# Transposes of 15 chunks as 32x32 blocks on DVE with copies on the DMA queues, instead of on PE

## The chip, the core and the metric

One NeuronCore of one Trainium2 chip runs the whole kernel. The metric is the device time of one execution in microseconds (us). Engines are named as in the profile: PE (TensorE matmuls), PEld (its weight loads), DVE (VectorE), ACT (ScalarE), POOL (GpSimd) and SP (SyncE, which issues all DMAs here from one queue, in order). A difference under 0.3% (2.9 us) is what a measurement of this kernel cannot tell from none.

## What is computed

Shapes: batch 4, 8 heads, sequence 576, head width 64, so 2304 tokens of width 512.

```python
x = attention(q, k, v)                       # local band of 7 plus a 4x down-sampled attention
# block 1: layer norm and a channel MLP of width 2048
xn = (x - mu) / sqrt(var + 1e-6) * g_ln
x2 = x + relu(xn @ w_ch1) @ w_ch2            # 512 -> 2048 -> 512
# block 2: token MLP of width 256 over the 576 tokens of a batch, then a channel MLP of width 1536
u  = x2 + (relu(x2.T @ w_tok1) @ w_tok2).T
out = u + relu(u @ w_ch1b) @ w_ch2b          # 512 -> 1536 -> 512
```

## The kernel before

The 2304 tokens are 18 tiles of 128, taken two at a time as **chunks** of 256. Block 1 works on chunks 0 to 8, block 2 on the same tokens as chunks 9 to 17. All large products run in fp32r on a high and a low part of each operand, three matmuls (`PASSES`) for one product.

The spine is a list of 252 **units**, one for each chunk and each 128 columns of the hidden width: 16 units a chunk in block 1 (`UA`), 12 in block 2 (`UB`). In a unit, `g1` does 12 matmuls of 256 columns into a PSUM tile `h`, ACT and DVE turn it into the high and low part of `ht` (ReLU), and `g2` does 6 matmuls of 512 columns that add into two accumulators. `g1` of the next unit is issued ahead of `g2` of this one, so `ht` has one unit's time to become ready. `base[c]` is the number of the first unit of chunk c.

`g1` needs the chunk's activations transposed, in `xT[c]` (128 channels by 4 by 2 parts by 256 tokens; two buffers, so chunk c can be written when the last `g1` of chunk c-2 has read). For each of the two tiles of a chunk, `xt_transpose` issues four 128x128 transposes on PE into one PSUM bank; `xt_hi` (ACT) writes the high part from there, `xt_lo` (DVE) the low part.

Everything else is hung into the spine by `put(pos, f)`, at a place counted in units: attention of the later batches (`LATER`), layer norm (`ln_center`), the token product of a batch (`tok1`, over 5 tiles of tokens, the fifth only 64 rows, then `tok_relu` and `tok2`), and the weights. Those are 64-bit in DRAM; `split_unit` turns each piece (128x512, two pieces to a unit) by three DVE steps, an ACT and a DVE step into high and low parts. The weights of block 2 (24 pieces, tensor `wb`) are loaded through two staging buffers `st` while chunks 8 and 9 run, since they take the buffers of block 1's weights as those come free.

`put` sets priorities; the framework's scheduler then places each instruction on its engine's queue when it expects its inputs to be there. Each engine, SP among them, runs its queue strictly in order. SP takes its DMAs' counters in turn from a set of eight.

Of the kernel before, what the change touches and what calls it, by code (L numbers as in the profile page):

```python
# [7 lines left out]
F32 = mybir.dt.float32  # L8
F32R = mybir.dt.float32r
I32 = mybir.dt.int32  # L10
ACTF = mybir.ActivationFunctionType
ALU = mybir.AluOpType
# [4 lines left out]
DM = H * D  # L17
# [3 lines left out]
CT = 2  # L21
CN = CT * 128
NCH = NTILE // CT
KD = DM // 128
# [7 lines left out]
DT = 256  # L32
# [2 lines left out]
QW = 512  # L35
T2P = 288
PASSES = ((0, 0), (0, 1), (1, 0))
XSP = 50
HP2 = 300
START_PAIRS = 5  # L40
SETS = 3
# [24 lines left out]
    td_copy 4 1  # L66
"""

LATER = ((1, 25), (27, 56), (57, 87))


def tile_of(b, tl):
    g = 9 * (b // 2)
    if tl == 4:
        return g + 4
    return g + tl + (5 if b % 2 else 0)
# [16 lines left out]
def block_kernel(ctx: ExitStack, tc: tile.TileContext, qk, vw, vg, g_ln, wa, t1, t2, wb, band, out):  # L93
    nc = tc.nc
# [7 lines left out]
    xt_p = ctx.enter_context(tc.tile_pool(name="xt_p", bufs=2))  # L102
    ht_p = ctx.enter_context(tc.tile_pool(name="ht_p", bufs=2))
    x_p = ctx.enter_context(tc.tile_pool(name="x_p", bufs=5))
# [9 lines left out]
    x2_scr = [dram.tile([128, CT, DM], F32, name=f"x2_scr{c}") for c in range(NCH)]  # L114
# [11 lines left out]
    def psg(tag=None):  # L126
        if tag is None:
            turn[0] += 1
            tag = rota[turn[0] % len(rota)]
        return POOLS[tag].tile([128, 512], F32, tag=tag, name=tag)  # L130

    def f32(ap):
        return ap.bitcast(F32)
# [5 lines left out]
    wa, wb, t1, t2 = (w.bitcast(I32) for w in (wa, wb, t1, t2))  # L139
# [392 lines left out]
    xT = {}  # L532
    mvs = {}
    rstd = {}
    xcs = {}
# [35 lines left out]
    def xt_transpose(c, j, src):  # L571
        ps = psg()
        for kk in range(KD):
            nc.tensor.transpose(ps[:, kk * 128:(kk + 1) * 128], src[:, kk * 128:(kk + 1) * 128], ident)  # L574
        xps[c, j] = ps.rearrange("p (k n) -> p k n", k=KD)

    def xt_hi(c, j):
        if c not in xT:
            xT[c] = xt_p.tile([128, KD, 2, CN], F32R, tag="xt", name="xt")
        n = slice(j * 128, (j + 1) * 128)  # L580
        nc.scalar.activation(out=xT[c][:, :, 0, n], in_=xps[c, j], func=ACTF.Copy)  # L581

    def xt_lo(c, j):
        n = slice(j * 128, (j + 1) * 128)
        nc.vector.tensor_tensor(  # L585
            out=xT[c][:, :, 1, n], in0=xps.pop((c, j)), in1=f32(xT[c][:, :, 0, n]), op=ALU.subtract
        )

    def xt_split(c, j):
        with tc.high_priority(offset=XSP):  # L590
            xt_hi(c, j)
            xt_lo(c, j)


    def nunits(c):
# [57 lines left out]
    uch = {}  # L653
    tokw = {}
# [29 lines left out]
    def xs_load(b, n):  # L684
        t = tok["pool"].tile([128, DM], F32, tag="xr", name="xr", bufs=1)
        k = tile_of(b, n)
        nc.sync.dma_start(out=t, in_=x2_scr[k // CT][:, k % CT])
        xs[b, n] = t

    def xs_split(b, n):  # L690
# [6 lines left out]
    rps = {}  # L697
    r_t = {}

    def tok1(b, n):  # L700
        t = xs.pop((b, n))
        rows = slice(64 * (b % 2), 64 * (b % 2) + 64) if n == 4 else slice(0, 128)
        for m in range(DT // 128):
            if n == 0:
                rps[b, m] = psg("k")
            for i, (a, e) in enumerate(PASSES):
                nc.tensor.matmul(  # L707
                    out=rps[b, m], lhsT=tokw["t1"][rows, a, n, m * 128:(m + 1) * 128], rhs=t[rows, e, :],
                    start=(n == 0 and i == 0), stop=(n == 4 and i == 2),
                )  # L710

    def tok_relu(b):
        r = wp.tile([128, DT // 128, 2, DM], F32R, tag="w", name="r")
# [39 lines left out]
    def put(pos, f, *args):  # L753
        u, half = divmod(int(2 * pos), 2)
        u = min(u, NSEQ - 1)
        (bg if half else mid)[u].append(lambda: f(*args))

    def put_prep1(c, e):
        for j in range(CT):
            put(e - 5.5 + j, ln_center, c, j)  # L760
            put(e - 3.5 + j, lambda c=c, j=j: xt_transpose(c, j, xcs.pop((c, j))))
            put(e - 3 + j, xt_split, c, j)
        put(e + 4, ln_rstd, c)

    def put_tok(b, u):
        for n in range(5):
            put(u + n, xs_load, b, n)
            put(u + 1 + n, xs_split, b, n)
            put(u + 2 + n, tok1, b, n)
        put(u + 6.5, tok_relu, b)  # L770

    def put_prep2(c, e):
        put(e - 7, u_load, c)
        for j in range(CT):
            put(e - 5 + 0.5 * j, tok2, c, j)
            put(e - 3.5 + j, lambda c=c, j=j: xt_transpose(c, j, uch[c][:, j]))
            put(e - 3 + j, xt_split, c, j)


    pieces = [(i, part) for i in range(UA) for part in range(NPC)]  # L780
# [54 lines left out]
    def conv_step(k):  # L835
# [6 lines left out]
    steps = {f.__name__: f for f in (  # L842
        q_sums, v_sums, s_max, s_exp, d_max, d_exp, t_pe, t_copy, td_pe, td_copy, avd_pe, avd_norm, up_write,
        up_read, av_pe, av_norm, load, fill, consts, ln_center, xt_pe, xt_hi, xt_lo,
    )}
    steps.update(
# [39 lines left out]
    for n in range(START_PAIRS, len(order) + 1):  # L886
        a = [(f, n) for f in (a_scores, a_down, a_turn, a_turn_down)] if n < len(order) else []
        v = [(f, n - 1) for f in (a_values_down, a_values)] if n > START_PAIRS else []
        later += a[:1] + v[:1] + a[1:2] + v[1:] + a[2:]
    o = 0  # L890
    for i, (u0, u1) in enumerate(LATER):
        e = later.index((a_values, NP * (i + 2) - 1)) + 1
        for k, (f, n) in enumerate(later[o:e]):
            put(u0 + k * (u1 - u0) / (e - o), f, n)
        o = e
    for c in range(2, NCH):
        put_prep1(c, base[c] - 1)
# [23 lines left out]
    for c in range(NCH, 2 * NCH):  # L921
        put_prep2(c, base[c] - 1)
# [97 lines left out]
```

## Time and profile before

| | |
|---|---|
| median of 3 runs | 961.3 us (960.32 to 963.04) |
| the profiled execution's own time | 960.96 us |
| its span in the profile | 958.8 us |
| mean granted clock of PE | 0.989 of 2.4 GHz |

The span is what the rows further down divide; 2.2 us lie around it.

### The profile page before, as it was taken

The page shows a single profiled execution, that of the slowest core. Times are in us where ns is not written, and L with a number is a line of the kernel's source. Part 1 is how long each engine was busy: PE and PEld are TensorE (multiplying, and loading weights), DVE is VectorE, ACT ScalarE, POOL GpSimd, SP SyncE. Part 2 cuts the span into 40 slices and gives each one's busy share as a digit, 9 for nine tenths or more (in the row PEclk, how much of TensorE's full clock was granted, in tenths as well). Part 3 has the DMA queues.
Part 4 walks back from the last instruction along what each step waited for, and adds up shares of the span by engine and source line. Part 5 has one row for each costly group of instructions (what it writes and reads, how often), then busy time and mean ns, then how long its engine had stood idle before and what let it go on. Part 6 is the DMA issues. An engine that isn't in the chain of part 4 may idle for free.

```text
span 958.8 us, 16724 instructions
## 1 busy us (share of the span) xinstructions
PE 926.9 (97%) x6822; PEld 813.5 (85%) x6822; DVE 430.8 (45%) x1014; ACT 279.5 (29%) x809; POOL 148.8 (16%) x176
## 2 busy tenths in 40 slices
PE   7978999899999999999999999999999999999998
PEld 5767788788988889888889988888888988899997
DVE  4786888873333423366322268982222213122211
ACT  5444354434433334332121123221121111111111
POOL 6453214312123220120110011001000010000000
PEclk9799999999999999999999999999999999999999
DMA  8654565632131320234110135531101010000000
GB/s 220 182 184 138 151 194 159 186 95 77 53 94 57 98 63 18 92 103 150 33 44 23 44 111 168 190 126 66 56 12 44 23 45 23 1 23 1 23 23 23
DMA packets 43932, 81.85 MB, mean 85 GB/s; under 512 B 4080, under 2 KB 22768, under 8 KB 43856
## 3 DMA queue, kind: packets, MB, share of 16 engines
q1 hardware_dynamic: 43856, 80.79, 27.1%
q8 instruction: 54, 0.88, 0.4%
q14 instruction: 22, 0.18, 0.1%
HBM read 66.62 MB, written 14.16 MB: 84 GB/s over the span
## 4 chain that ended last, share of the span: by engine, by line
PE 76%; DMA 10%; DVE 9%; ACT 2%; issue 1%; POOL 1%; SPq 1%; DVEq 0%; ACTq 0%; POOLq 0%
PE h L615 31%; PE acc L636 30%; DMA st<-in_wb_dram 3%; PE g L738 2%; DVE cv L160 2%; PE k L707 2%; DMA xr<-x_scr 2%; PE k L636 2%; DMA up_scr<-od 2%; DVE cv L155 1%; DVE w L168 1%; PE g L574 1%; PE g L283 1%; PE g L364 1%; PE g L469 1%
## 5 line engine op out<-in xcount | busy, mean ns | idle before, releaser
L615 PEld LDWEIGHTS h<-xt,w 128*128 128x128 f32 x3024 | 396.5, 191 | 25.2 <-ACT w L165 1.9
L615 PE MATMUL h<-xt,w 128*128 128x256 f32 x3024 | 414.2, 285 | 2.3 <-ACT w L165 1.7
L636 PE MATMUL acc<-w,ht 128*128 128x512 f32 x1416 | 380.6, 400 | 7.3 <-ACT ht L621 4.3
L636 PEld LDWEIGHTS acc<-w,ht 128*128 128x128 f32 x1416 | 251.9, 189 | 59.8 <-ACT ht L621 6.2
L622 DVE SCALAR_TENSOR_TENSOR ht<-h,ht 128x256 fp32r<-128x256 f32 x252 | 106.1, 422 | 411.7 <-ACT ht L621 411.4
L621 ACT ACTIVATE ht<-h 128x256 fp32r<-128x256 f32 x252 | 96.6, 384 | 433.0 <-PE h L615 423.2
L694 POOL TENSOR_TENSOR xs<-xr,xs 128x512 fp32r<-128x512 f32 x20 | 27.6, 1380 | 338.3 <-ACT xs L693 338.3
L347 POOL TENSOR_TENSOR vg<-vg 72x256 f32<-72x256 f32 x39 | 31.6, 810 | 168.7 <-DMA vg<-in_vg_dram 129.7
L165 ACT ACTIVATE w<-cv 128x512 fp32r<-128x512 f32 x56 | 35.5, 634 | 72.4 <-DVE cv L160 72.2
L168 DVE TENSOR_TENSOR w<-cv,w 128x512 fp32r<-128x512 f32 x56 | 43.2, 775 | 9.4 <-ACT w L165 9.2
L155 DVE SCALAR_TENSOR_TENSOR cv<-st,cv 128x512 int32<-128x512 int32 (+4 forms) x63 | 42.8, 682 | 0.8
L160 DVE SCALAR_TENSOR_TENSOR cv<-st,cv 128x512 int32<-128x512 int32 (+4 forms) x63 | 42.4, 675 | 0.6
L516 POOL TENSOR_TENSOR x<-x,pt 128x256 f32<-128x256 f32 (+2 forms) x44 | 28.1, 651 | 65.6 <-ACT pt L503 55.7
L707 PE MATMUL k<-xs,t1w 128*128 128x512 f32 (+1 forms) x120 | 35.7, 404 | 0.0
L738 PE MATMUL g<-r,t2w 128*128 128x512 f32 x120 | 34.4, 396 | 0.0
L150 DVE TENSOR_SCALAR cv<-st 128x512 int32<-128x512 int32 (+4 forms) x63 | 25.5, 406 | 12.8 <-DMA st<-in_wb_dram 6.2
L636 PE MATMUL k<-w,ht 128*128 128x512 f32 x96 | 27.7, 406 | 0.1
L585 DVE TENSOR_TENSOR xt<-g,xt 128x512 fp32r<-128x512 f32 x28 | 19.2, 687 | 12.9 <-ACT xt L581 12.3
L707 PEld LDWEIGHTS k<-xs,t1w 128*128 128x128 f32 (+1 forms) x120 | 20.6, 188 | 3.9 <-issue 0.6
L503 ACT ACTIVATE pt<-g,rz 128x64 f32<-128x64 f32 (+1 forms) x78 | 17.5, 323 | 21.9 <-DVE rz L493 21.8
L738 PEld LDWEIGHTS g<-r,t2w 128*128 128x128 f32 x120 | 21.0, 189 | 3.2 <-issue 0.2
L301 ACT ACTIVATE sm<-g,nm 128x70 f32<-128x70 f32 x80 | 18.1, 349 | 12.1 <-DVE nm L293 12.1
(162 smaller groups left out, 713.7 us busy)
## 6 DMA issues: line engine op xcount, KB each, us to landing
st<-in_wa_dram SPq DMA_DIRECT2D x28, 512.0 KB
st<-in_wb_dram SPq DMA_DIRECT2D x24, 512.0 KB
qk<-in_qk_dram SPq DMA_DIRECT2D x13, 579.0 KB
xr<-x_scr SPq DMA_DIRECT2D x20, 256.0 KB
x_scr<-x SPq DMA_DIRECT2D x18, 256.0 KB
x<-x_scr SPq DMA_DIRECT2D x9, 512.0 KB
out_dram<-x SPq DMA_DIRECT2D x18, 256.0 KB
vw<-in_vw_dram SPq DMA_DIRECT2D x13, 319.9 KB
```

The costliest lines, as they stand in the source:

```text
L155: nc.vector.scalar_tensor_tensor(out=f, in0=h, scalar=-0x40000000, in1=f, op0=ALU.bitwise_and, op1=ALU.bitwise_or)
L160: nc.vector.scalar_tensor_tensor(out=f, in0=l, scalar=29, in1=f, op0=ALU.logical_shift_right, op1=ALU.bitwise_or)
L165: nc.scalar.activation(out=hi, in_=f.bitcast(F32), func=ACTF.Copy)
L168: nc.vector.tensor_tensor(out=lo, in0=f.bitcast(F32), in1=f32(hi), op=ALU.subtract)
L347: nc.gpsimd.tensor_tensor(out=vd[:, :, :, :D], in0=vd[:, :, :, :D], in1=vgt[:, :, o:o + 128].rearrange("p c (h d) -> p c h d", h=2), op=AL ...
L516: (eng or nc.gpsimd).tensor_tensor(out=x, in0=x, in1=tmp[rows, tl:tl + k].rearrange("p t h d -> p t (h d)"), op=ALU.add)
L615: nc.tensor.matmul(out=hp[:, :CN], lhsT=w[:, 0, a, kk * 128:(kk + 1) * 128], rhs=xT[c][:, kk, e, :], start=(n == 0), stop=(n == 3 * KD - 1),)
L621: nc.scalar.activation(out=t[:, 0], in_=hp[:, :CN], func=ACTF.Relu)
L622: nc.vector.scalar_tensor_tensor(out=t[:, 1], in0=hp[:, :CN], scalar=0.0, in1=f32(t[:, 0]), op0=ALU.max, op1=ALU.subtract)
L636: nc.tensor.matmul(out=acc[c, j], lhsT=t[:, a, j * 128:(j + 1) * 128], rhs=w[:, 1, e, :], start=(m == 0 and n == 0), stop=(last and n == 2),)
L707: nc.tensor.matmul(out=rps[b, m], lhsT=tokw["t1"][rows, a, n, m * 128:(m + 1) * 128], rhs=t[rows, e, :], start=(n == 0 and i == 0), stop=( ...
L738: nc.tensor.matmul(out=ps, lhsT=tokw["t2"][:, a, m, o:o + 128], rhs=r_t[b][:, m, e, :], start=(i == 0), stop=(i == len(ops) - 1),)
```

## The change

- Chunks 3 to 17 are no longer transposed on PE. `xt_turn` transposes a 128x512 tile on DVE, which turns each 32x32 block in its place. Sixteen DMAs then carry the blocks to where the full transpose wants them: each takes 32 partitions by 4 pieces of 32 words (16 KB in pieces of 128 bytes) into the low half of `xT[c]`. `xt_part` makes the high part on ACT and subtracts it on DVE, in place. Chunks 0 to 2 stay on PE.
- To leave time for the copies, `ln_center` (block 1) and `tok2` (block 2) of a chunk are put 5.5 to 6 units earlier, and attention of batches 2 and 3 is drawn together in time (`LATER`).
- The fifth tile of `tok1`: both halves of the partitions get the same 64 tokens (two DMAs), and the two hidden halves m = 0 and 1 use rows 0 to 63 and 64 to 127 of PE, in turns.

```diff
-LATER = ((1, 25), (27, 56), (57, 87))
+LATER = ((1, 25), (26, 51), (52, 82))
+    def xt_turn(c, j, src):
+        t = xcs.pop((c, j)) if src is None else x_p.tile([128, DM], F32, tag="xc", name="xc", bufs=2)
+        nc.vector.transpose(out=t, in_=t if src is None else src)
+        if c not in xT:
+            xT[c] = xt_p.tile([128, KD, 2, CN], F32R, tag="xt", name="xt")
+        blocks = t.rearrange("p (k q n) -> p k q n", k=KD, q=4)
+        for i in range(4):
+            n = j * 128 + 32 * i
+            for q in range(4):
+                nc.sync.dma_start(
+                    out=f32(xT[c])[32 * q:32 * q + 32, :, 1, n:n + 32], in_=blocks[32 * i:32 * i + 32, :, q, :]
+                )
+    def xt_part(c, j):
+        n = slice(j * 128, (j + 1) * 128)
+        hi, lo = xT[c][:, :, 0, n], xT[c][:, :, 1, n]
+        nc.scalar.activation(out=hi, in_=f32(lo), func=ACTF.Copy)
+        nc.vector.tensor_tensor(out=lo, in0=f32(lo), in1=f32(hi), op=ALU.subtract)
...
-        rows = slice(64 * (b % 2), 64 * (b % 2) + 64) if n == 4 else slice(0, 128)
...
+        for i, m in [(i, m) for i in range(3) for m in M] if n == 4 else [(i, m) for m in M for i in range(3)]:
+            a, e = PASSES[i]
+            rows = slice(64 * m, 64 * m + 64) if n == 4 else slice(0, 128)
...
     def put_prep1(c, e):
-            put(e - 5.5 + j, ln_center, c, j)
-            put(e - 3.5 + j, lambda c=c, j=j: xt_transpose(c, j, xcs.pop((c, j))))
-            put(e - 3 + j, xt_split, c, j)
+                put(e - 11.5 + j, ln_center, c, j)
+                put(e - 10.5 + j, xt_turn, c, j, None)
+                put(e - 3 + j, xt_part, c, j)
...
     def put_prep2(c, e):
-            put(e - 5 + 0.5 * j, tok2, c, j)
-            put(e - 3.5 + j, lambda c=c, j=j: xt_transpose(c, j, uch[c][:, j]))
-            put(e - 3 + j, xt_split, c, j)
+            put(e - 11 + 0.5 * j, tok2, c, j)
+            put(e - 10 + 0.5 * j, lambda c=c, j=j: xt_turn(c, j, uch[c][:, j]))
+            put(e - 3 + j, xt_part, c, j)
```

How the order on the engines moves. First PE, at one place in chunk 11 (`h` is a `g1`, `acc` a `g2`; `x` is the chunk's tile). Before:

```order
L615 MATMUL h<-xt,w 128x256 x12
L574 MATMUL g<-ident,x 128x128
L636 MATMUL acc<-w,ht 128x512 x6
L574 MATMUL g<-ident,x 128x128
L615 MATMUL h<-xt,w 128x256 x12
L574 MATMUL g<-ident,x 128x128 x2
L636 MATMUL acc<-w,ht 128x512 x6
L574 MATMUL g<-ident,x 128x128 x2
```

and PE of the changed kernel in chunk 9, the stage in which the weights of block 2 are still being made:

```order
L629 MATMUL h<-xt,w 128x256 x12
L760 MATMUL g<-r,t2w 128x512 x11
L629 MATMUL h<-xt,w 128x256 x9
L650 MATMUL acc<-w,ht 128x512 x3
L629 MATMUL h<-xt,w 128x256
L650 MATMUL acc<-w,ht 128x512 x3
```

The transposes are gone, and `tok2` (`t2w`) and `tok1` (`t1w`) of later chunks have come into chunk 9: from its first `g1` to the first of chunk 10 stand 24 matmuls of `tok1` and 30 of `tok2`, before 7 and 18, and 14 transposes. In chunk 8 it is 30 and 30 against 33, 24 and 8 transposes.

Next SP's queue where block 2's weights are loaded (`st<-in_wb`), towards the end of chunk 8; `xt` is the `xT` of chunk 10, `xr` a tile for `tok1`, `x2_scr` the output of block 1. Before:

```order
L191 DMA st_6573<-in_wb_dram 128x1024
L191 DMA st_6581<-in_wb_dram 128x1024
L191 DMA st_6623<-in_wb_dram 128x1024
L191 DMA st_6631<-in_wb_dram 128x1024
L191 DMA st_6673<-in_wb_dram 128x1024
L650 DMA x2_scr8_114<-x_3995 128x512 x2
```

Changed, with what each entry waits for (DMAHW is a counter of an earlier DMA):

```order
L190 DMA st_6822<-in_wb_dram 128x1024 [waits DMAHW6_49,DVE_49]
L586 DMA xt_7163<-xc_7161 32x4x32 [waits PE_49]
L586 DMA xt_7163<-xc_7161 32x4x32 x4
L586 DMA xt_7163<-xc_7161 32x4x32 [waits DMAHW7_49]
L586 DMA xt_7163<-xc_7161 32x4x32 [waits DMAHW0_49]
L190 DMA st_6830<-in_wb_dram 128x1024 [waits DMAHW1_49,DVE_49]
L586 DMA xt_7163<-xc_7161 32x4x32 [waits DMAHW2_49]
L586 DMA xt_7163<-xc_7161 32x4x32 [waits DMAHW3_49]
L664 DMA x2_scr8_114<-x_3931 128x512 [waits DMAHW4_49,DVE_49]
```

The copies stand among the loads; those of chunk 10 wait for the last `g1` of chunk 8, and the 14th of the 24 loads stands behind seven of them. Before, 15 loads had been issued when chunk 8's output was stored; now 13 stand ahead of that wait.

Last DVE, from the end of chunk 9 on: `L662` adds chunk 9's result, `L636` is the `ht` of a unit, `L579` the transpose of chunk 12's tiles, `L594` the subtraction of chunk 11's:

```order
L662 TENSOR_TENSOR x_6476<-acc_7129,x_6476 128x512
L662 TENSOR_TENSOR x_6476<-acc_7133,x_6476 128x512
L636 SCALAR_TENSOR_TENSOR ht_7447<-h_7434,ht_7447 128x256
L765 TENSOR_TENSOR x_8133<-g_8193,x_8133 128x512
L636 SCALAR_TENSOR_TENSOR ht_7493<-h_7480,ht_7493 128x256
L579 STREAM_TRANSPOSE xc_7827<-x_7741 128x512
L594 TENSOR_TENSOR xt_7498<-xt_7498 128x4x128
L636 SCALAR_TENSOR_TENSOR ht_7552<-h_7539,ht_7552 128x256
L636 SCALAR_TENSOR_TENSOR ht_7574<-h_7561,ht_7574 128x256
```

The subtraction of a tile stands behind the `ht` of the third unit of chunk 10 and ahead of the fourth, so `ht` waits behind it when the sixteen copies of the tile are late. SP's queue holds these copies, and among them the two stores of chunk 9's output, in the same order.

## Rows read from the trace of the kernel before

**Rows 1.** The page's first part: busy time of each engine and its share.

```profile
PE 926.9 (97%) x6822; PEld 813.5 (85%) x6822; DVE 430.8 (45%) x1014; ACT 279.5 (29%) x809; POOL 148.8 (16%) x176
```

**Rows 2.** Busy time by engine in four stretches, then PE clock, DMA share, GB/s.

```profile
0.00:206.00 206.00, 181.94 (x1658) 152.95 (x1659) 155.92 (x350) 92.55 (x283) 75.64 (x89) 0.95 0.55 165
206.00:558.00 352.00, 350.56 (x2754) 311.16 (x2753) 127.59 (x387) 108.02 (x347) 55.18 (x74) 1.00 0.23 71
558.00:649.00 91.00, 88.72 (x521) 76.16 (x520) 76.31 (x137) 28.97 (x61) 8.98 (x6) 1.00 0.49 157
649.00:958.80 309.80, 305.64 (x1895) 273.20 (x1893) 70.93 (x142) 49.92 (x119) 9.01 (x7) 1.00 0.08 28
```

**Rows 3.** Timeline of PE in chunk 5: start, length, line, instruction, count.

```profile
415.75 1.60 PE L615 MATMUL h<-xt,w 128*128 128x256 f32 x12
417.18 0.60 PE L574 MATMUL g<-ident,xc 128*128 128x128 f32 x4
...
419.00 1.60 PE L615 MATMUL h<-xt,w 128*128 128x256 f32 x12
...
421.82 1.59 PE L615 MATMUL h<-xt,w 128*128 128x256 f32 x12
```

**Rows 4.** Timeline of PE over a full and the half tile of the token product.

```profile
572.66 1.56 PE L707 MATMUL k<-xs,t1w 128*128 128x512 f32 x6
574.06 1.55 PE L636 MATMUL acc<-w,ht 128*128 128x512 f32 x6
...
576.97 1.65 PE L707 MATMUL k<-xs,t1w 64*128 64x512 f32 x6
578.55 1.66 PE L636 MATMUL acc<-w,ht 128*128 128x512 f32 x6
```

**Rows 5.** Timeline of PE: 64x64 matmuls of the attention scores, alternately on both row halves.

```profile
229.44 0.27 PE L283 MATMUL k<-qk 64*64 64x70 f32 x1
...
229.46 0.27 PE L283 MATMUL g<-qk 64*64 64x70 f32 x1
229.55 0.22 PE L283 MATMUL k<-qk 64*64 64x70 f32 x1
```

**Rows 6.** Groups of instructions: busy us, mean ns of one, idle before and its releasers.

```profile
L168 DVE TENSOR_TENSOR w<-cv,w 128x512 fp32r<-128x512 f32 x56 | 43.2, 775 | 9.4 <-ACT w L165 9.2
L585 DVE TENSOR_TENSOR xt<-g,xt 128x512 fp32r<-128x512 f32 x28 | 19.2, 687 | 12.9 <-ACT xt L581 12.3
L581 ACT ACTIVATE xt<-g 128x512 fp32r<-128x512 f32 x28 | 16.8, 603 | 9.4 <-PE g L574 9.3
```

**Rows 7.** Two lines that issue DMAs: ns of one issue on SP, minimum/median/maximum.

```profile
L440 SPq DMA_DIRECT2D x<-up_scr x16: 497/504/1509, 30.1 to 412.6; - x16
L429 SPq DMA_DIRECT2D up_scr<-od x26: 777/808/988, 20.0 to 409.1; - x26
```

**Rows 8.** Timeline of SP's DMA issues around one hand-over through DRAM.

```profile
235.24 1.67 SPq L429 DMA_DIRECT2D up_scr<-od  x2
238.70 1.78 SPq L444 DMA_DIRECT2D x<-up_scr  x3
240.53 0.50 SPq L440 DMA_DIRECT2D x<-up_scr  x1
```

**Rows 9.** Busy time in the stretch of those reads, as rows 2.

```profile
238.70:242.00 3.30, 3.30 (x24) 3.04 (x23) 0.42 (x1) 0.63 (x2) 3.30 (x5) 1.00 0.33 93
```

**Rows 10.** The chain that ended last, two of its loads of block 2's weights.

```profile
583.16 4.25 DMA st<-in_wb_dram
...
605.05 4.59 DMA st<-in_wb_dram
```

**Rows 11.** Timeline of DVE: the last step on the last piece of those weights.

```profile
645.64 0.69 DVE L168 TENSOR_TENSOR w<-cv,w 128x512 fp32r<-128x512 f32 x1 [0.36 <-ACT w L165]
```

**Rows 12.** Timeline of PE: the `g2` that reads that piece.

```profile
647.74 1.63 PE L636 MATMUL acc<-w,ht 128*128 128x512 f32 x6
```

**Rows 13.** Waits from 555 to 655 us: us in total, times, longest.

```profile
PE g L574 <- DVE x L743: 0.7, 2, 0.4
```

More of the change, by code (lines that the diff above doesn't have):

```diff
@@ L37 @@
 PASSES = ((0, 0), (0, 1), (1, 0))
-XSP = 50
 HP2 = 300
@@ L587, in xt_lo @@
         )
[L589 to L592, printed above, removed]
     def nunits(c):
@@ L686, in xs_load @@
         k = tile_of(b, n)
-        nc.sync.dma_start(out=t, in_=x2_scr[k // CT][:, k % CT])
+        if n == 4:
+            o = 64 * (b % 2)
+            for m in range(2):
+                nc.sync.dma_start(out=t[64 * m:64 * m + 64], in_=x2_scr[k // CT][o:o + 64, k % CT])
+        else:
+            nc.sync.dma_start(out=t, in_=x2_scr[k // CT][:, k % CT])
         xs[b, n] = t
@@ L701, in tok1 @@
         t = xs.pop((b, n))
-        rows = slice(64 * (b % 2), 64 * (b % 2) + 64) if n == 4 else slice(0, 128)
-        for m in range(DT // 128):
-            if n == 0:
+        M = range(DT // 128)
+        if n == 0:
+            for m in M:
                 rps[b, m] = psg("k")
[L706 to L710, printed above, removed]
+        for i, m in [(i, m) for i in range(3) for m in M] if n == 4 else [(i, m) for m in M for i in range(3)]:
+            a, e = PASSES[i]
+            rows = slice(64 * m, 64 * m + 64) if n == 4 else slice(0, 128)
+            nc.tensor.matmul(
+                out=rps[b, m], lhsT=tokw["t1"][rows, a, n, m * 128:(m + 1) * 128], rhs=t[rows, e, :],
+                start=(n == 0 and i == 0), stop=(n == 4 and i == 2),
+            )
     def tok_relu(b):
@@ L759, in put_prep1 @@
         for j in range(CT):
-            put(e - 5.5 + j, ln_center, c, j)
-            put(e - 3.5 + j, lambda c=c, j=j: xt_transpose(c, j, xcs.pop((c, j))))
-            put(e - 3 + j, xt_split, c, j)
+            if c == 2:
+                put(e - 5.5 + j, ln_center, c, j)
+                put(e - 3.5 + j, xt_pe, c, j)
+                put(e - 3 + j, xt_hi, c, j)
+                put(e - 3 + j, xt_lo, c, j)
+            else:
+                put(e - 11.5 + j, ln_center, c, j)
+                put(e - 10.5 + j, xt_turn, c, j, None)
+                put(e - 3 + j, xt_part, c, j)
         put(e + 4, ln_rstd, c)
@@ L772, in put_prep2 @@
     def put_prep2(c, e):
-        put(e - 7, u_load, c)
+        put(e - 12.5, u_load, c)
         for j in range(CT):
-            put(e - 5 + 0.5 * j, tok2, c, j)
-            put(e - 3.5 + j, lambda c=c, j=j: xt_transpose(c, j, uch[c][:, j]))
-            put(e - 3 + j, xt_split, c, j)
+            put(e - 11 + 0.5 * j, tok2, c, j)
+            put(e - 10 + 0.5 * j, lambda c=c, j=j: xt_turn(c, j, uch[c][:, j]))
+            put(e - 3 + j, xt_part, c, j)
     pieces = [(i, part) for i in range(UA) for part in range(NPC)]
```

## The prediction

> **What bounds the kernel now.** I read the page's first part first: PE is busy 97% of the span, DVE 45%, ACT 29% [rows 1]. A share is an average over stages, so next comes the busy time in four stretches [rows 2]. From 206 to 558 us PE is idle for 1.4 of 352 us, and from 649 to the end for 4.2 of 310 us, most of that the tail; the granted clock is 1.00 of 2.4 GHz in both. There each matmul taken from PE shortens the kernel by its own time. From 0 to 206 us weights are made and attention runs; the change begins behind that (chunks 0 to 2 stay). The stretch from 558 to 649 us, in which the weights of block 2 are made, is the doubtful one: PE is idle only 2.3 of 91 us, but what it reads is ready barely in time. The last piece of the weights is finished at 645.64 + 0.69 = 646.33 us [rows 11], and the `g2` that reads it starts at 647.74 [rows 12]: 1.4 us of margin.
>
> **What is removed from PE.** The timeline of chunk 5 gives the price. Two plain units follow each other by 421.82 - 419.00 = 2.82 us; the unit with one tile's four transposes inside takes 419.00 - 415.75 = 3.25 us [rows 3]. So a tile costs 0.43 us of PE, and four transposes alone 0.11 each. Fifteen chunks have 30 tiles: 30 x 0.43 = **-12.9 us** (with the 0.46 that the line's rounding allows, -13.8). Waits of PE ahead of transposes go too: -0.7 us [rows 13].
>
> **The half tile of tok1.** A full tile's six matmuls take 574.06 - 572.66 = 1.40 us, or 0.233 each. The half tile has 64 rows and still takes 578.55 - 576.97 = 1.58 us [rows 4], since a matmul's time does not go by its rows. In turns on the two row halves, two matmuls could run at once. That PE does this the trace shows: 64x64 matmuls of the attention scores, alternately on the halves, start 0.02 us apart, and the next 0.1 us on, though one is given 0.27 us [rows 5]. Three pairs of 0.26 are 0.78 us: 0.8 saved, four batches, **-3.2 us** (bounds 0, if they run one by one, and -3.5). The second load of 64 rows is one more DMA of 0.50 us [rows 7] a batch, issued with the first, and its bytes are written beside the first's: nothing. The Trainium skill, page "TensorEngine Tiling (Array Packing)", section "Theoretical Speedup", allows up to 2x for an operand of at most 64 rows; its "Key Properties" adds that a switch of tiling mode drains PE, which would speak against a whole gain. The half tile's 1.58 against 1.40 agrees with a price at the switch, paid before as after, so it does not enter my sum.
>
> **What is added to DVE and ACT.** A DVE transpose of 128x512 is not in this trace. Below, it costs nothing; the nearest rows are a subtraction from PSUM at 687 ns and one from SBUF at 775 ns [rows 6]. I take 0.7 us, with twice that as the upper end. Thirty are 21 us (0 to 42) on an engine that has about half its time free; in the PE-bound stretches DVE is busy 128 of 352 and 71 of 310 us [rows 2]. The subtraction costs 0.78 in place of 0.69, 30 x 0.09 = 2.7 us, and ACT's copy stays near its 0.60 [rows 6]. Cover: `ht` has a unit of 2.82 us to become ready, and one transpose ahead of it takes a quarter of that. Without that cover it would be 30 x 0.7 = 21 us, more than the gain. Cost taken: 0.
>
> **What is added to SP and the DMA queues.** Sixteen copies for each of 30 tiles, 480 in all. One issue on SP takes 0.50 us for a copy of 64 rows of 512 bytes and 0.81 for one in 288 pieces [rows 7]; one in 256 pieces takes 1.78 / 3 = 0.59, and the last landing of two issues that ended at 236.91 releases a read at 238.70, 1.8 us later [rows 8]. A copy here has 128 pieces, nearest to the 0.50: I take s = **0.50 us**, ends 0 and 0.81. That is 240 us of SP's queue. Bytes are no limit: 512-byte pieces move at 93 GB/s at a share of 0.33 [rows 9], so 282 GB/s in full, 29 ns a piece on each of 16 queues; eight pieces a queue, 0.23 us a copy, less than its issue.
>
> What waits for them is the subtraction (`L594`), which stands in DVE's order ahead of the `ht` of the fourth unit of a chunk. The copies can begin when the last `g1` of the chunk two back has read `xT`. From there to that place are three units and most of a `g2`, 3 x 2.82 + 0.8 = 9.3 us, and one more unit of slack until `g2` lacks its `ht`: **12.1 us**. The copies take, with the two stores among them, 18 x 0.50 + 1.8 = 10.8 us. They fit, with 1.3 us to spare. The second tile has four more units (11.3 us) for 16 x 0.50 = 8.0. ACT's copy of the high part waits in the same way ahead of its share of `ht`, by the same times. Cost taken: 0; this is the step I trust least.
>
> **What is only moved.** `ln_center`, `tok2`, the load of `u` and attention (`LATER`) keep their instructions and stand some 6 units earlier. Where PE is never idle, the order of its work costs nothing; at the price of a wait, the places are PE's gaps of 1.4 us up to 558 us [rows 2], which such work may fill or widen: 0, within 1 us.
>
> **The stage of block 2's weights.** A piece goes load, ACT and DVE, and the two staging buffers make it one loop: between two loads of the chain, six pieces apart, lie 605.05 - 583.16 = 21.9 us, 3.65 us a piece [rows 10]. SP's order now has 13 loads ahead of chunk 8's store where it had 15, and seven copies ahead of the 14th. So the last weights come up to 2 x 3.65 + 7 x 0.50 = 10.8 us later. Against that, chunk 9 gets other work for PE: 54 matmuls of the token product at 0.233 (12.6 us) where 25 of these and 14 transposes at 0.11 stood (7.3 us), 5.3 us more. That is drawn forward, not added. What is left idle is 7.3 - 5.3 = 2.0 without the price of the copies, 5.5 with it; I take the middle, **+3.7 us**. Bounds: 0 (the margin of 1.4 covers the smaller one nearly) and +11 (six transposes and three subtractions, nine times 0.7, stand inside the loop as well, though DVE has 14.7 us idle in the stretch).
>
> **Sum.** -12.9 - 0.7 - 3.2 + 3.7 = -13.1. The profiled execution took 960.96 us (span 958.8 and 2.2 around it), 0.3 below the median; 960.96 - 13.1 = 947.9, and with the 0.3 **948 us**.
>
> **Rivals.**
> 1. *The halves of tok1 run one after another.* Only a row of smaller matmuls speaks for concurrency. Then +3.2: 951 us.
> 2. *The weight stage loses the whole upper end.* The 2 pieces' delay and the nine DVE steps add up: 948 + 7.3 = 955 us. For it: the margin of 1.4 us. Against it: DVE's idle time there.
> 3. *Copies late in DVE's order* (the slower side). If s is over (12.1 - 1.8) / 18 = 0.57, the subtraction holds `ht`, and PE stands still in each of 15 chunks. The gain of 13.1 is 0.87 us a chunk, so it decides at s = (12.1 + 0.87 - 1.8) / 18 = 0.62. At the 0.59 of the copy in 256 pieces, 12.4 us, the loss is 0.3 x 15 = 4.5 (952); at 0.81 it is 16.4, 4.3 late, 64 us: 1012 us. For it: both dearer issues are of many pieces, as these are. Against it: 128 pieces are half as many as the 0.59 had.
> 4. *Copies are served one at a time.* At 1.8 us from issue to landing, 16 take 29 us, two tiles 58 against the 34 of a 12-unit chunk (45 of a 16-unit one): 9 x 24 + 6 x 13 = 294, some 1240 us. Against it: four transfers of the same stretch are issued within 241.03 - 238.70 = 2.3 us [rows 8], none waiting for the one before. The Trainium skill, page "DMA: Bandwidth & Descriptors", section "Rules for kernel authors", says that a transfer under 64 KB is mostly overhead and should be coalesced, and a copy here has 16 KB; by that rule it would go this way, and the trace speaks against it wherever transfers overlap.
>
> **How the numbers follow.** Chances: the forecast as it stands, 943 to 953 us, 0.55; rival 1, 0.08; rival 2, 0.12 (0.09 of it still faster, 0.03 within the measurement); rival 3, 0.22 (0.03 faster, 0.05 within, 0.14 slower); rival 4, 0.03. Low end: -13.8 - 3.5 - 0.7 and nothing for the weights is -18.0, **942 us** with the measurement's spread. High end: rivals 1 and 2 together reach 959; the mild part of rival 3 reaches 963, and beyond **963** and below 942 I leave 0.2. A measurement of this kernel can tell about 0.3% (2.9 us). Faster by more than that: 0.55 + 0.08 + 0.09 + 0.03 = **0.75**. Within it: 0.03 + 0.05 = **0.08**. Slower: 0.14 + 0.03 = **0.17**.
>
> **What would show it.** In the busy time of 206 to 558 and 649 to the end, units of 2.82 us follow each other without a gap, and no transpose of chunks 3 to 17 is on PE. The half tile of `tok1` takes 0.8 us. The issue of a copy on SP is near 0.50 us, and the wait of DVE's `L594` for its DMA ends before `ht` is wanted: PE waiting for `ht` behind such a wait, once a chunk, makes the forecast wrong, by rival 3. Between chunk 8's store and the last weights, PE is idle 2 + 4 us, named as a wait for `w`; more is rival 2. Copies that each begin when the last has landed are rival 4.

## Result and the profile after

The changed kernel takes 951.0 us (median of 6 runs, 949.2 to 952.3) against 960.05 us for the kernel before on the same chip (6 runs, 958.9 to 963.0): a ratio of 0.990, 95% interval 0.988 to 0.992. That is faster by 9.1 us, about two thirds of the 13 us of the forecast; 948 us had been forecast, 942 to 963 us as the range. The profiled execution's span is 950.5 us.

The page's first part of the changed kernel answers to [rows 1]:

```profile
PE 916.2 (96%) x6702; PEld 801.0 (84%) x6702; DVE 447.9 (47%) x1044; ACT 280.6 (30%) x809; POOL 147.5 (16%) x176
```

PE has 120 matmuls less, those of 30 tiles, and is busy 10.7 us less; DVE is busy 17 us more for 30 more instructions. The busy time in the stretches of [rows 2] (columns as there):

```profile
0.00:206.00 206.00, 181.43 (x1665) 152.05 (x1666) 152.84 (x348) 92.07 (x282) 75.51 (x89) 0.95 0.55 165
206.00:558.00 352.00, 350.24 (x2701) 309.00 (x2701) 137.12 (x403) 108.82 (x348) 54.47 (x74) 1.00 0.29 80
558.00:649.00 91.00, 87.23 (x491) 73.48 (x489) 76.86 (x134) 28.07 (x57) 9.76 (x7) 1.00 0.56 168
649.00:950.50 301.50, 297.32 (x1849) 266.50 (x1848) 81.11 (x161) 51.63 (x124) 7.76 (x6) 1.00 0.16 41
```

PE is still never idle for long: 1.8 us in the second stretch, 4.2 in the last (the tail, as before). In the third, where the weights of block 2 are made, its idle time went from 2.3 to 3.8 us.

Stretches of fixed times hold different work in the two kernels, so the next table cuts at the first `g1` of a chunk instead. It is worked out from the PE rows of the traces: us between the cuts and, in brackets, PE's idle time there (without the 5 to 6 us before PE's first instruction). Each line is one execution.

```
                 chunks 0 to 6   chunks 7 to 10   chunks 11 to 17
before           494.7 (19.6)    190.0 (2.3)      274.2 (4.2)
changed          495.5 (20.7)    197.1 (3.8)      257.9 (4.1)
moves_alone      496.3 (19.5)    191.0 (2.7)      272.2 (4.1)
later_alone      498.2 (17.6)    190.0 (2.3)      274.2 (4.2)
mid              491.8 (21.8)    199.9 (5.1)      257.9 (4.1)
mid_wstage       489.3 (19.2)    188.9 (2.1)      267.9 (4.6)
```

(The lower four are experiments, below.) All of the gain lies from chunk 7 on: 190.0 + 274.2 = 464.2 became 455.0 us. Up to there nothing is gained, though 48 of the 120 transposes are gone, some 5 us of PE. A cut at the first `g1` of chunk 2 tells more: up to it the changed kernel falls 5.2 us behind (210.8 against 205.6 us), with 50 more attention matmuls on PE; from it to chunk 7 it takes 4.4 us less (284.7 against 289.1), with 48 transposes and 50 attention matmuls fewer and 3 matmuls of the token product more. Twelve tiles at 0.43 us are 5.2 us, less 0.7 for the 3 matmuls: in these two traces the swap pays its price there, and the attention matmuls that came forward shortened next to nothing behind. From chunk 7 to 10 the changed kernel takes longer because work of the token product comes earlier, and from chunk 11 on it takes less, because that work and the transposes are missing there.

### The profile page after: what moved, and what is told of

Read it like the earlier page. It is cut to its first block, busy times and chain, and to the rows that moved or that the text cites. A ratio compares the mean times of both kernels' runs of the same rounds, so it can differ in the third digit from the quotient of the medians.

```text
span 950.5 us, 17304 instructions
## 1 busy us (share of the span) xinstructions
PE 916.2 (96%) x6702; PEld 801.0 (84%) x6702; DVE 447.9 (47%) x1044; ACT 280.6 (30%) x809; POOL 147.5 (16%) x176
## 4 chain that ended last, share of the span: by engine, by line
PE 78%; DVE 8%; DMA 8%; SPq 2%; ACT 1%; issue 1%; POOL 1%; DVEq 0%; ACTq 0%
PE h L629 33%; PE acc L650 31%; DMA up_scr<-od 2%; DMA st<-in_wb_dram 2%; PE k L650 2%; PE k L729 2%; SPq L586 2%; DMA xr<-x_scr 2%; DVE cv L159 2%; PE g L760 2%; DVE cv L154 1%; PE g L282 1%; PE g L363 1%; PE g L318 1%; PE g L468 1%
## 5 line engine op out<-in xcount | busy, mean ns | idle before, releaser
L636 DVE SCALAR_TENSOR_TENSOR ht<-h,ht 128x256 fp32r<-128x256 f32 x252 | 105.8, 421 | 354.6 <-ACT ht L635 354.3
L729 PE MATMUL k<-xs,t1w 128*128 128x512 f32 (+1 forms) x120 | 33.5, 410 | 2.2 <-ACT xs L713 1.4
L593 ACT ACTIVATE xt<-xt 128x512 fp32r<-128x512 f32 x30 | 19.0, 632 | 50.0 <-DMA xt<-xc 49.9
L594 DVE TENSOR_TENSOR xt<-xt 128x512 fp32r<-128x512 f32 x30 | 20.6, 686 | 23.6 <-ACT xt L593 23.5
```

What stands on the lines that cost most here:

```text
L636: nc.vector.scalar_tensor_tensor(out=t[:, 1], in0=hp[:, :CN], scalar=0.0, in1=f32(t[:, 0]), op0=ALU.max, op1=ALU.subtract)
L729: nc.tensor.matmul(out=rps[b, m], lhsT=tokw["t1"][rows, a, n, m * 128:(m + 1) * 128], rhs=t[rows, e, :], start=(n == 0 and i == 0), stop=( ...
```

## Experiments

Each was timed against the kernel before on the same chip. 0.1% is 0.96 us. Two theories stood at the start. **Theory A**: the engine swap (transposes from PE to DVE and DMA) gives what was forecast, and the missing 4 us lie in the two other edits: the half tile, and the moves (`LATER`, and the earlier places of layer norm and `tok2`). **The rival**: the moves are free and the copies eat the 4 us, on SP's queue or in waits on DVE and ACT.

### The parts one by one

**tok1_alone** is the kernel before with `xs_load` and `tok1` as in the change. 

> The kernel before, with the half tile of the token product on both row halves and nothing else. Theory A (the pairs run at once, but the order tears some of them apart, as in the changed kernel, where the 24 matmuls take 5.0 us against 7.1): 2 to 2.5 us less than before, 957.8 us. Rival (the whole -3.2 of the forecast is to be had): 956.8. If the halves ran one by one: 960.

**turn_alone** is the changed kernel with both as before. 

> The changed kernel with the half tile of the token product as it was before. Theory A: 2 to 2.5 us more than the changed kernel, 953.3 us. Rival (most of the gain comes from the half tile, and the turn on DVE and DMA gives nearly nothing): 957 or more.

**moves_alone** keeps everything but the swap:

```diff
-                put(e - 10.5 + j, xt_turn, c, j, None)
-                put(e - 3 + j, xt_part, c, j)
+                put(e - 3.5 + j, xt_pe, c, j)
+                put(e - 3 + j, xt_split, c, j)
...
-            put(e - 10 + 0.5 * j, lambda c=c, j=j: xt_turn(c, j, uch[c][:, j]))
-            put(e - 3 + j, xt_part, c, j)
+            put(e - 3.5 + j, lambda c=c, j=j: xt_transpose(c, j, uch[c][:, j]))
+            put(e - 3 + j, xt_split, c, j)
```

> The changed kernel with the transposes of all chunks on PE again, at their old places; what stays are the earlier places of layer norm and tok2, the attention drawn together, and the half tile. Theory A (the moves cost 2 to 4 us of PE, by attention matmuls between others and by waits, and this is what the forecast lacked): 960 us, no faster than before. Rival B (the moves are free, and the 4 us lie with the copies and DVE): 957.8, that of the half tile alone.

Measured: tok1_alone 959.3 us, ratio 0.9986 (0.9969 to 1.0004); turn_alone 953.9, 0.9922 (0.9897 to 0.9947); moves_alone 961.2, 1.0001 (0.9983 to 1.0018). So the half tile is worth 1.3 us alone, less than either theory of its run had, and 2.0 us inside the changed kernel (0.9922 against 0.9901). Neither is clear of noise by its interval; the traces' own rows say 1.5 us alone (from the start of each of the 24 matmuls to the next on PE, 7.12 us before and 5.65 us in tok1_alone). The moves take that back: the kernel that has them and the half tile is no faster than before. The swap itself, moves_alone against changed, is 1.0001 - 0.9901 = 1.0%, 9.6 us (some 2.5 either way by the two intervals). That bears out theory A and not its rival.

**later_alone** is the kernel before with one line of the change:

```diff
-LATER = ((1, 25), (27, 56), (57, 87))
+LATER = ((1, 25), (26, 51), (52, 82))
```

> The kernel before, with only the attention of the later batches drawn together in time (LATER). Theory A (this alone costs the 2 us by which the kernel with the moves and the transposes on PE fell behind that with the half tile alone, 961.2 against 959.3, since matmuls drawn ahead of chunk 3 lengthen it by more than they shorten the chunks behind): 962.5 us. Rival (the earlier layer norm and tok2 cost it, or the two runs differ by chance): 960.5, as before.

Measured: 962.3 us, ratio 1.0026 (1.0009 to 1.0043): slower by 2.5 us. The interval stays above 1, so drawing attention together costs something by itself, as theory A had it.

**later_old** is the changed kernel with that line as before. Layer norm of the chunks of batches 2 and 3 then stands ahead of the last attention of these batches, so it works on an `x` that is not complete. 

> The changed kernel with attention of the later batches at its old places in time. Theory A (drawing it together costs PE some 2 us between 136 and 270 us): 949 us. Rival B (it costs nothing): 951, as changed. Rival C (the old places collide with the earlier layer norm, which waits for that attention): over 953.

Measured: 952.7 us, ratio 0.9910 (0.9877 to 0.9942). Nothing that can be told came back, and the interval leaves room for each of the three forecasts. PE waits longer for ACT between 206 and 560 us than in the changed kernel (3.6 us against 0.6; us in total, times, longest), which fits rival C without showing it:

```profile
PE acc L650 <- ACT ht L635: 3.6, 2, 2.5
```

**later_late** is the changed kernel with batch 2's attention at (30, 51). 

> The changed kernel with attention of batch 2 beginning at unit 30 instead of 26, and ending at 51 as changed: denser, but fewer of its matmuls come into chunks 0 and 1. Theory A (what LATER costs, 2.8 us on its own, is paid by the matmuls drawn into chunks 0 and 1, which take longer there by 4.4 us and give back 0.9 behind): 949 us. Rival (density costs it, by more switches between matmul shapes): 951 or more.

Measured: 951.3 us, 0.9895 (0.9874 to 0.9916), no gain that can be told, though the interval still holds the 949 of theory A. Up to chunk 2 it was 9 us ahead of the changed kernel in its trace (201.5 against 210.8 us), with 86 attention matmuls fewer, and from there to chunk 7 it lost 7 us of it (291.7 against 284.7). Most of what chunks 0 and 1 no longer paid, chunks 2 to 6 paid; the place of the cost is not settled by this run.

**mid** draws attention together less, and gives the copies less time for it:

```diff
-LATER = ((1, 25), (26, 51), (52, 82))
+LATER = ((1, 25), (27, 54), (55, 85))
...
-                put(e - 11.5 + j, ln_center, c, j)
-                put(e - 10.5 + j, xt_turn, c, j, None)
+                put(e - 8.5 + j, ln_center, c, j)
+                put(e - 7.5 + j, xt_turn, c, j, None)
```

> The changed kernel with layer norm and the turn of block 1 three units later (8.5 and 7.5 units ahead instead of 11.5 and 10.5), and so attention of batches 2 and 3 at (27, 54) and (55, 85), nearly its old places. The copies have three units (8.5 us) less: a tile's sixteen, 10.8 us with landing, are still done before its subtraction three units ahead. Theory A (of the moves' 2 to 3 us most comes back): 949 us. Rival (the copies then come late, or the stretch is not what costs): 951 or more.

Measured: 949.1 us, 0.9874 (0.9852 to 0.9896), 2.6 us better than changed by the medians of the ratios, though the intervals overlap. In its trace chunks 0 to 6 became shorter and chunks 7 to 10 longer (table above, 491.8 against 495.5 and 199.9 against 197.1).

### The copies

**four_copies** carries each block within its partitions, so it leaves out what the full transpose needs and shows only the price of the issues:

```diff
-            for q in range(4):
-                nc.sync.dma_start(
-                    out=f32(xT[c])[32 * q:32 * q + 32, :, 1, n:n + 32], in_=blocks[32 * i:32 * i + 32, :, q, :]
-                )
+            nc.sync.dma_start(out=f32(xT[c])[:, :, 1, n:n + 32], in_=blocks[:, :, i, :])
```

> The changed kernel with four copies of 64 KB a tile in place of sixteen of 16 KB: the blocks are not carried to other partitions, so what follows works on activations that are not fully transposed; the work of PE, ACT and DVE and the bytes are the same. 360 issues on SP are gone. Theory A (the copies are hidden but for the stage of block 2's weights): 949 to 951 us. Rival (the copies cost time in every chunk, by waits on ACT and DVE or on SP's queue): 946 or less.

**thirtytwo_copies** cuts each copy in two (`for k in (0, 2)`, on pieces `k:k + 2`). 

> The changed kernel with each copy cut in two: 32 a tile of 8 KB, the same bytes. At the 0.60 us of one issue in the changed kernel's trace, a chunk's 64 copies and two stores take 39.6 us; with landing, ACT and DVE 43 us from the last read of the buffer to the next first use, against 33.8 us of a chunk of 12 units and 45 of one of 16. Theory A (the issue on SP is the price, hidden only as long as it fits into a chunk): 9 us for each of nine chunks, some 1030 us. Rival (what counts is bytes or the landing, not the issue): within 5 us of 951.

Measured: four_copies 949.6 us, 0.9892 (0.9866 to 0.9917); thirtytwo_copies 1056.8 us, 1.1012 (1.0980 to 1.1043). To take away 360 of 480 issues gains 0.9 us, nothing that can be told; to add 480 costs 106 us. Bytes are the same in both. The extra issues cost nothing in chunks 2 to 7, of 16 units each (328.7 us in the trace against 329.8 in the changed kernel's), and some 10 us a chunk in chunks 10 to 16, of 12 units. So the copies are hidden as long as their issues fit into a chunk, and are the bound as soon as they don't. The line that issues them, in the kernel with 32 (ns of one issue, minimum/median/maximum), and the largest wait of PE there (us in total, times, longest):

```profile
L587 SPq DMA_DIRECT2D xt<-xc x960: 585/595/1739, 202.8 to 1011.3; - x192
```

```profile
PE h L631 <- ACT xt L595: 72.0, 8, 21.9
```

PE waits for the transposed operand itself, up to 21.9 us at once. The forecast's nine chunks were nearly right in sum: chunks 9 to 17 take 79.7 us more than in the changed kernel's trace, 81 had been forecast. What lies beyond the forecast's 1030 us is chunk 8, with 87.5 us against 59.4: the wait of 21.9 us stands at its end, behind copies that share SP's queue with the weights of block 2. What of the two holds it there no run separates. After such waits the granted clock is lower too, 0.949 in the mean of these runs against 0.987 in the changed kernel's. The Trainium skill, page "DMA: Bandwidth & Descriptors", section "Rules for kernel authors", would have small transfers like these coalesced. The traces agree that such a copy is mostly overhead: one of 16 KB takes SP 0.60 us, one of 64 KB 0.64. But coalescing them gave no time that could be measured here, since the sixteen were hidden already.

**wstage_pe** is the changed kernel with chunks 9, 10 and 11 on PE in `put_prep2` (`if c in (9, 10, 11):` the two lines of moves_alone, else those of the change). 

> The changed kernel with chunks 9, 10 and 11 transposed on PE, as before, so that no copy stands among the loads of block 2's weights and DVE has six transposes less there. Theory A (the copies cost that stage only the 1.5 us of more idle PE that the trace shows): 6 x 0.43 = 2.6 us come back, 1.5 go, 952 us. Rival (the stage loses the 3.7 us of the forecast, or more, to the copies): 950 or less.

Measured: 950.1 us, 0.9901 (0.9869 to 0.9933), the ratio of the changed kernel. That interval holds both forecasts (0.992 and 0.990), so the times alone do not decide. The traces do better: from the first `g1` of chunk 7 to the end both kernels take 455.0 us, though six tiles are back on PE, 2.6 us by the price of a tile. So the swap had cost the stage about that, of which 1.7 us are idle PE (7.9 us from chunk 7 on against 6.2). Its waits of PE from 555 to 655 us hold no wait for `xs` any more:

```profile
PE acc L655 <- ACT ht L640: 1.4, 1, 1.4
PE acc L655 <- DVE ht L641: 0.7, 1, 0.7
```

The changed kernel in the same stretch:

```profile
PE k L729 <- ACT xs L713: 1.4, 1, 1.4
PE acc L650 <- ACT ht L635: 0.8, 1, 0.8
PE k L729 <- POOL xs L714: 0.7, 1, 0.7
PE acc L650 <- DVE ht L636: 0.7, 2, 0.5
```

For 2.1 of 3.6 us PE waits there for the token product's operand, drawn forward, and never for the weights.

### The half tile, and a better version

**tok1_together** pins the half tile's matmuls in the order in which they are written, and the first of the next `g2` behind them:

```diff
+            if n == 4:
+                tc.keep_in_program_order(mm)
+                pin[:] = [True]
...
+                if pin:
+                    tc.keep_in_program_order(mm)
+                    pin.clear()
```

> The changed kernel with the six matmuls of each half tile kept in the order they are written in, after the g1 and ahead of the g2 between which they are written, so that the three pairs stand together. In the changed kernel's trace a half tile in one piece takes 0.91 us, one torn apart up to 1.7. Theory A: 24 matmuls in 3.7 instead of 5.0 us, and fewer switches for what follows: 950 us, 1.3 less. Rival (pinning makes PE wait where the half tile is not yet ready): over 952.

Measured: 961.0 us, 1.0009 (0.9993 to 1.0025): ten microseconds lost, the rival. The pinned matmuls wait for their operand with all of PE's queue behind them. Timeline of PE there (start, length, line, instruction, count, idle before and its releaser):

```profile
591.97 3.43 PE L733 MATMUL k<-xs,t1w 128*128 128x512 f32 x6 [6.07 <-ACT xs L717]
597.32 0.79 PE L733 MATMUL k<-xs,t1w 64*128 64x512 f32 x2 [1.92 <-ACT xs L717]
598.67 1.22 PE L733 MATMUL k<-xs,t1w 64*128 64x512 f32 x4 [0.55 <-POOL xs L718]
599.82 2.93 PE L651 MATMUL acc<-w,ht 128*128 128x512 f32 x6
```

and the busy time of these stretches, the granted clock third from the end:

```profile
560.00:590.00 30.00, 25.90 (x153) 22.54 (x151) 24.51 (x43) 8.64 (x16) 1.29 (x1) 0.99 0.51 131
590.00:597.00 7.00, 3.29 (x6) 1.66 (x6) 3.87 (x7) 1.62 (x3) 1.27 (x1) 0.50 0.62 213
597.00:604.00 7.00, 5.42 (x14) 2.90 (x14) 5.42 (x7) 3.13 (x7) 2.54 (x2) 0.56 0.72 224
604.00:612.00 8.00, 7.97 (x40) 6.41 (x40) 7.96 (x14) 2.33 (x5) 1.57 (x1) 1.00 0.35 110
```

The wait of 6 us, from 585.9 to 592.0, is paid twice: from 590 to 597 us the granted clock is 0.50 of 2.4 GHz, to 604 us 0.56, and six matmuls of `g2` take 2.9 us instead of 1.6.

**mid_wstage** is mid and wstage_pe together. 

> The last two edits that were no slower than the changed kernel, together: layer norm and the turn of block 1 three units later with attention nearly at its old places (ratio to before 0.9874 on its own), and chunks 9 to 11 on PE (0.9901, as changed). Theory A (the first gives back what the moves cost, the second clears the stage of block 2's weights; they lie in different stretches and add up): 947.5 to 949 us, a ratio of 0.987. Rival (0.9874 against 0.9901 was chance, and the second is no gain): 951, 0.990.

Measured: 946.0 us, ratio 0.9866 (0.9843 to 0.9888), the best of all: 12.6 us faster than before. Against the changed kernel (0.9883 to 0.9920) it is 3.4 us better by the ratios, with intervals that still just touch. Against mid alone (0.9874) it is 0.8 us better, which cannot be told; that the two gains add up is not shown.

## Why the prediction was right in direction and 3 us off in size

**The price of a transpose: right.** From chunk 11 on, where nothing waits, the changed kernel takes 16.3 us less. In those PE rows stand 48 transposes, 37 matmuls of the token product and 6 of its half tile less; at 0.23 us the 37 are 8.6 us, and the half tiles take 3.36 less 1.32 = 2.0 us less by their own rows (from the start of each to the next on PE). That leaves 5.6 us for 12 tiles, 0.47 each; 0.43 was taken, with 0.46 at its end.

**DVE: right.** The transpose takes 0.71 us (0.7 was taken), the subtraction 0.69 (0.78 taken). Both lines in the changed kernel (ns of one, minimum/median/maximum):

```profile
L579 DVE STREAM_TRANSPOSE xc<-x x18: 698/712/714, 559.3 to 865.8; 128x512 f32<-128x512 f32 x18
L594 DVE TENSOR_TENSOR xt<-xt x30: 649/691/695, 227.2 to 901.8; 128x512 fp32r<-128x512 f32 x30
```

**The copies: hidden as forecast, by a margin that was mis-sized twice.** The issue was taken as 0.50 us and is 0.60:

```profile
L586 SPq DMA_DIRECT2D xt<-xc x480: 585/599/1564, 205.8 to 899.0; - x160
```

By the forecast's own limit (0.57) the copies should have come late: at 0.60 they take 18 x 0.60 + 1.8 = 12.6 us where 12.1 were given, 0.5 x 15 = 7.5 us lost. They did not, because the slack of 12.1 us was too small as well. That the second error outweighed the first was luck. In chunk 15 the trace shows all of it. SP's queue, then ACT, DVE and PE:

```profile
842.21 4.45 SPq L586 DMA_DIRECT2D xt<-xc  x7
846.88 0.41 SPq L664 DMA_DIRECT2D out_dram<-x  x1
847.34 0.58 SPq L586 DMA_DIRECT2D xt<-xc  x1
848.02 0.54 SPq L664 DMA_DIRECT2D out_dram<-x  x1
848.61 15.74 SPq L586 DMA_DIRECT2D xt<-xc  x24
```

```profile
855.10 0.63 ACT L593 ACTIVATE xt<-xt 128x512 fp32r<-128x512 f32 x1 [1.27 <-DMA xt<-xc]
```

```profile
855.76 0.69 DVE L594 TENSOR_TENSOR xt<-xt 128x512 fp32r<-128x512 f32 x1
856.68 0.42 DVE L636 SCALAR_TENSOR_TENSOR ht<-h,ht 128x256 fp32r<-128x256 f32 x1 [0.22 <-ACT ht L635]
```

```profile
854.63 1.59 PE L629 MATMUL h<-xt,w 128*128 128x256 f32 x12
856.06 1.55 PE L650 MATMUL acc<-w,ht 128*128 128x512 f32 x6
857.45 1.59 PE L629 MATMUL h<-xt,w 128*128 128x256 f32 x12
858.88 1.55 PE L650 MATMUL acc<-w,ht 128*128 128x512 f32 x6
```

The sixteenth copy is issued near 848.61 + 8 x 0.66 = 853.9 and releases ACT at 855.10, 12.9 us after the first issue; 10.8 had been forecast. The `ht` behind the subtraction is of the fifth unit, not of the fourth, and is wanted by the `g2` at 858.88. It is ready at 857.1. From the first issue to where `ht` would be late are 16.3 us, not 12.1: the forecast's place was read in chunk 10 and its units counted without the work that stands between them. So ACT does wait for the copy, and PE doesn't: 858.88 - 857.1 = 1.8 us are left, 0.1 us for each of the 18 issues. An estimate from these rows puts the limit at some 0.75 us from one issue to the next; thirtytwo_copies, with two issues of 0.66 in place of one, goes beyond it.

**The half tile: right in its mechanism, its size off.** The term was -3.2 us and came out as -1.3 (alone) to -2.0 (in place). The pairs do run at once; where the six stand together, they take 654.51 - 653.60 = 0.91 us where 1.58 were taken before [rows 4]:

```profile
653.60 0.98 PE L729 MATMUL k<-xs,t1w 64*128 64x512 f32 x6
654.51 1.65 PE L650 MATMUL acc<-w,ht 128*128 128x512 f32 x6
```

But of the four half tiles the order tears three apart (other matmuls stand between their pairs), two of them even within a pair. One of these two:

```profile
472.87 0.50 PE L729 MATMUL k<-xs,t1w 64*128 64x512 f32 x2
...
475.40 0.50 PE L729 MATMUL k<-xs,t1w 64*128 64x512 f32 x1
475.83 1.67 PE L650 MATMUL acc<-w,ht 128*128 128x512 f32 x6
```

The single one takes 0.43 us until the next, nearly as long as two matmuls of 128 rows. By the starts of all 24 rows the half tiles took 7.1 us before and 5.0 us after, 2.1 less. The step of the prediction that failed was to price a tile in one piece, three pairs of 0.26 us, without looking at how it stands in the order. The Trainium skill, page "TensorEngine Tiling (Array Packing)", section "Key Properties", has the drain at a change of tiling mode; the 0.43 us of a lone matmul agrees, and a torn tile pays it several times.

**What is only moved: wrong.** It was priced at 0, within 1 us, "where PE is never idle, the order of its work costs nothing". moves_alone against tok1_alone says +1.4 us (1.0001 against 0.9986), later_alone +2.5 us for the attention alone. That drawing attention together costs time is shown by later_alone; where the cost sits is not. PE is busy with attention 3.6 us longer in the changed kernel's trace than before (139.0 against 135.4 us), and chunks 0 and 1 lengthen by more than the later chunks shorten (above). But two kernels with attention at the same places, before and tok1_alone, differ by 1.5 us in this, and up to 206 us the granted clock differs between executions of such kernels (0.93 to 0.96 of 2.4 GHz over that stretch), which is as much. Two tries at its place, later_old and later_late, did not settle it; mid, which undoes about half of the drawing together, gives back 2.6 us by the ratios, not clear of noise.

**The weight stage: right in kind, rather too dear.** +3.7 was taken. PE's idle time grew by 1.5 us, and undoing the swap there was worth about 2.6 us, by the two traces. It was mostly `xs` that came late and never, as the text expected, `w`.

**Sum.** Swap -9.6 (forecast -12.9 - 0.7 + 3.7 = -9.9), half tile -1.3 (-3.2), moves +1.4 (0): -9.5, for 9.1 to 9.5 measured. The forecast was 13.1. Two terms account for the difference, the half tile and the moves. The runs were made so that these three add up to the ratio of the changed kernel; the sum is no check by itself, and each of the terms has an interval of some 2 us either way. One thing that none of the forecast's terms holds is the clock: the six executions of the changed kernel had a mean granted clock of 0.987 (0.986 to 0.989), the 68 executions of the kernel before that were timed beside the experiments 0.989 (0.984 to 0.995). By an estimate that is 0.002 of 951, some 2 us, within the -9.6 of the swap; what lowers it is open.

## What to carry to other kernels

Where one engine is busy 97% of the time, work can be moved to idle engines even by a clumsy route: 480 small copies cost nothing that could be told as long as the queue that issues them is done before an in-order reader blocks something, and 106 us as soon as it isn't; so count issues per stretch against the time of that stretch, not bytes. Price what has to be moved to make room for such an edit as a part of the edit; here it took back as much as the second edit gave. An instruction that is cheap only next to its partner must be looked up in the order, but to force the order is worse if its operand can be late.

## What the runs showed of the hardware

- A DMA of 32 partitions by 4 pieces of 128 bytes costs SP 0.60 us, and one follows the other at 0.66 us; half as many pieces cost the same 0.60. A copy of 128 partitions by 4 pieces of 128 bytes costs 0.64 us (median of 120 in four_copies). Among these copies the price goes by the DMA, hardly by its size; a load of 512 KB of weights in the changed kernel costs SP 0.33 us.
- In tok1_together PE stood still from 585.9 to 592.0 us. Its granted clock was 0.50 of 2.4 GHz from 590 to 597 us, 0.56 from there to 604, and 1.00 behind that.
- A 64-row matmul alone between 128-row ones takes 0.43 us, two of them on different row halves take the same 0.43 (473.30 - 472.87).
